# The last short unit's first layer between the last tile's layers, its second layer in two column halves

## The chip, the cores and the metric

The kernel runs on one core of one Trainium2 chip. The metric is the device time of one execution in microseconds. The times of runs are medians; the profile shows one execution, in microseconds from its first instruction.

## The reference

Two stages follow each other. The first is causal attention with a decay, for 8 batches of 8 heads with 576 positions and 64 values per head. The second is a feed-forward block over the 4608 resulting rows.

```python
def _attn_ref(q, k, v, f):                       # 8 batches, 8 heads, 576 x 64
    scores = scale * np.matmul(q, k.transpose(0, 1, 3, 2))
    cum = np.cumsum(np.log(np.clip(f, 0.0001, 1.0)), axis=-1)
    decay = cum[:, :, :, None] - cum[:, :, None, :]
    scores = np.where(causal, -1000000000.0, scores + decay)
    attn = np.exp(scores - np.max(scores, axis=-1, keepdims=True))
    attn = attn / (np.sum(attn, axis=-1, keepdims=True) + 1e-09)
    return np.matmul(attn, v)

def _moe_ref(x, w_in, w_out):                    # x: 4608 x 512, d_ff = 2048
    h = x @ w_in
    g = h * np.clip(h + 3.0, 0.0, 6.0) / 6.0
    return g @ w_out
```

## The kernel before

All matrix products of the second stage are done in float16 with each operand split into a high and a low half; a product is then three matmuls: high x high, high x low and low x high.

Attention goes head by head (64 heads, in the order of the list `VH`). The feed-forward work is cut into units that are filled in between the attention's instructions. A batch has 576 positions: 512 of them make one *tile* (`moe_tile`, 8 in all), and the 64 positions left over of two batches together make one *short unit* of 128 positions (`moe_short`, 4 in all; the unit u serves batches 2u and 2u + 1).

A tile has two layers. The first (`h_unit`, 16 times, one for each block of 128 hidden values) multiplies weights by the tile's 512 positions: 4 x 3 matmuls of 512 columns into one PSUM tile `ph`, then a relu on ScalarE, a min-and-multiply on VectorE that reads `ph` again and so frees it, a cast on ScalarE to the high half and a subtraction on VectorE to the low half. Both halves lie in `gT`. The second layer (`out_unit`, 4 times, one for each 128 positions) sums over all 16 blocks: 16 x 3 matmuls of 512 columns (lines 819, 820, 821: the first two read the high half of `gT`, the third the low half) into one PSUM tile `po`, an eviction by ScalarE into an SBUF tile `o` (line 825), and a DMA to the output on SyncE's queue (line 828).

A short unit has the same two layers at 128 positions. Its first layer (`h_short`) is done in four groups of four blocks; a group is 4 x 4 x 3 matmuls of 128 columns (lines 797 to 799) into one PSUM tile `phs`, two relus (line 805, one for each batch's half), one min-and-multiply (line 809, which frees the PSUM tile), a cast (line 811) and a subtraction (line 812). Before, it writes into columns 0 to 127 of `gT`, which the out_unit of the same positions of the tile has read. Its second layer is one out_unit, whose rows go to the output in two DMAs.

PSUM tiles for this work come from three places: two buffers of `ps_m` and one of `ps_t`, taken by a counter (`mm_tile`: every third goes to `ps_t`). There are three buffers for the results of the relu (`rt`) and two for `o`.

The order of instructions on each engine is written by the framework's planner before the run: among those that are ready it takes the lowest priority number. The units are Python generators, and `fill` draws them piece by piece, from one `yield` to the next; a piece of an out_unit is six matmuls, a piece of an h_short is 24. Each piece is drawn in a priority block of its own, with `LOW_M = 0`:

```python
while credit[0] >= 1 and units:
    with tc.high_priority(offset=-LOW_M):
        r = next(units[0], 0)
```

After the last head the list `units` still holds what is left of the seventh tile; then the eighth tile (`t` = 7) and the last short unit (`u` = 3) are put behind it by `done`, and the loop `while units: fill(1)` draws them to the end.

The tile `vst` holds the batch's v in float32 (5 x 520 values per partition). Its readers are `v_scale` and `v_split`; the last `v_split` of the last batch is called at its sixth head.

Of the kernel before, what the change touches and what calls it, by code (L numbers as in the profile page):

```python
# [9 lines left out]
F16 = mybir.dt.float16  # L10
BF16 = mybir.dt.bfloat16
F32 = mybir.dt.float32
F32R = mybir.dt.float32r
I32 = mybir.dt.int32
AF = mybir.ActivationFunctionType
# [5 lines left out]
def kernel(  # L21
# [10 lines left out]
    nc = tc.nc  # L32

    NHEAD, D, S = qk.shape
    D //= 2
    B = vS.shape[0]
    H = NHEAD // B
    NT, DM = out.shape
    DFF = w_in.shape[1]
    P = 128  # L40
# [5 lines left out]
    NFC = DFF // P  # L46
    TT = 512
# [7 lines left out]
    p2 = ctx.enter_context(tc.tile_pool(name="p2", bufs=2))  # L55
# [22 lines left out]
        out=W[:, 4 * P:], in_=W[:, 4 * P:], pattern=[[-1, P]],  # L78
# [16 lines left out]
    QA = 256  # L95
# [35 lines left out]
    vst = cpool.tile([P, NCH, VR], F32, name="vst")  # L131

    w1 = [cpool.tile([P, NCC, DFF], F16, name=f"w1{i}") for i in range(2)]
    w2 = cpool.tile([P, NFC + 1, 2, DM], F16, name="w2")
    gT = cpool.tile([P, 2, NFC, TT], F16, name="gT")
# [15 lines left out]
    NG = 4  # L151
    SC = cpool.tile([P, 80], F32, name="SC")
    SV, IV, UO, UX, A1 = 0, 8, 16, 24, 32
# [47 lines left out]
    def scol(c):  # L201
        return SC[:, c:c + 1]
# [172 lines left out]
    def moe_scale_in(b, j):  # L375
        nc.vector.scalar_tensor_tensor(
            scol(A1 + NG * b + j), scol(IV + b), CG, scol(I1 + j), op0=ALU.mult, op1=ALU.mult
        )

    def moe_scale_out(b):  # L380
        nc.vector.scalar_tensor_tensor(
            scol(UO + b), scol(IV + b), 1.0 / (6.0 * CG), scol(I1R), op0=ALU.mult, op1=ALU.mult
        )
        nc.vector.tensor_tensor(scol(UO + b), scol(UO + b), scol(I2), op=ALU.mult)
        if b % 2 == 1:
            nc.vector.tensor_copy(SC[:64, UX + b:UX + b + 1], SC[:64, UO + b - 1:UO + b])
            nc.vector.tensor_copy(SC[64:, UX + b:UX + b + 1], SC[64:, UO + b:UO + b + 1])
# [191 lines left out]
    for half in NAT:  # L579
        g = [0]  # L580
# [3 lines left out]
    o = 0  # L584
# [176 lines left out]
    def mm_tile(name, three):  # L761

        turn[0] += 1
        if three and turn[0] % 3 == 0:
            return ps_t.tile([P, TT], F32, tag="tr", name=name)
        return ps_m.tile([P, TT], F32, tag="mm", name=name)

    def h_unit(t, fc, c0, c1):
        x = xT[t % 2]
        nw = c1 - c0  # L770
        ph = mm_tile(f"ph_{t}_{fc}_{c0}", t > 0 or c0 > 0)[:, :nw]
        fs_ = slice(fc * P, (fc + 1) * P)
        for cc in range(NCC):
            xh, xl = (x[:, cc, c0 // P:c1 // P, hl] for hl in range(2))
            nc.tensor.matmul(ph, w1[0][:, cc, fs_], xh, start=(cc == 0), stop=False)  # L775
            nc.tensor.matmul(ph, w1[0][:, cc, fs_], xl, start=False, stop=False)  # L776
            nc.tensor.matmul(ph, w1[1][:, cc, fs_], xh, start=False, stop=(cc == NCC - 1))  # L777
            if cc == 1 and nw == TT:
                yield H_COST
        r = p2.tile([P, TT], F32, tag="rt", name=f"r_{t}_{fc}_{c0}", bufs=3)[:, :nw]  # L780
        nc.scalar.activation(  # L781
            r, ph, AF.Relu, bias=bias_r, scale=scol(A1 + NG * t + fc * NG // NFC)
        )
        nc.vector.scalar_tensor_tensor(r, r, 6.0 * CG, ph, op0=ALU.min, op1=ALU.mult)  # L784
        nc.scalar.copy(gT[:, 0, fc, c0:c1], r)  # L785
        nc.vector.tensor_tensor(gT[:, 1, fc, c0:c1], r, gT[:, 0, fc, c0:c1], op=ALU.subtract)  # L786
        yield H_COST

    def h_short(u, j):
        x = xS[u % 2]  # L790
        n = NFC // NG
        ph = mm_tile(f"phs_{u}_{j}", True).rearrange("p (f t) -> p f t", f=n)
        for i in range(n):
            fs_ = slice((n * j + i) * P, (n * j + i + 1) * P)
            for cc in range(NCC):
                xh, xl = (x[:, cc, :, hl] for hl in range(2))
                nc.tensor.matmul(ph[:, i], w1[0][:, cc, fs_], xh, start=(cc == 0), stop=False)
                nc.tensor.matmul(ph[:, i], w1[0][:, cc, fs_], xl, start=False, stop=False)
                nc.tensor.matmul(ph[:, i], w1[1][:, cc, fs_], xh, start=False, stop=(cc == NCC - 1))
            if i == 1:  # L800
                yield H_COST
        r = p2.tile([P, TT], F32, tag="rt", name=f"rs_{u}_{j}", bufs=3)
        r = r.rearrange("p (f t) -> p f t", f=n)
        for h in range(2):
            nc.scalar.activation(
                r[:, :, 64 * h:64 * h + 64], ph[:, :, 64 * h:64 * h + 64], AF.Relu, bias=bias_r,
                scale=scol(A1 + NG * (2 * u + h) + j),
            )
        nc.vector.scalar_tensor_tensor(r, r, 6.0 * CG, ph, op0=ALU.min, op1=ALU.mult)
        g = [gT[:, i, n * j:n * j + n, 0:P] for i in range(2)]  # L810
        nc.scalar.copy(g[0], r)  # L811
        nc.vector.tensor_tensor(g[1], r, g[0], op=ALU.subtract)
        yield H_COST

    def out_unit(s, three, col, rows_):
        po = mm_tile(f"po_{rows_[0]}", three)
        ts_ = slice(s * P, (s + 1) * P)
        for fc in range(NFC):
            nc.tensor.matmul(po, gT[:, 0, fc, ts_], w2[:, fc, 0, :], start=(fc == 0), stop=False)  # L819
            nc.tensor.matmul(po, gT[:, 0, fc, ts_], w2[:, fc, 1, :], start=False, stop=False)  # L820
            nc.tensor.matmul(po, gT[:, 1, fc, ts_], w2[:, fc, 0, :], start=False, stop=(fc == NFC - 1))  # L821
            if fc % 2 and fc < NFC - 1:
                yield 2.0 - H_COST
        o = p2.tile([P, DM], F32, tag="o", name=f"o_{rows_[0]}")
        nc.scalar.activation(o, po, AF.Copy, scale=scol(col))
        w = P // len(rows_)
        for i, r0 in enumerate(rows_):
            nc.sync.dma_start(out[r0:r0 + w, :], o[i * w:(i + 1) * w])
        yield 2.0 - H_COST

    def moe_tile(t, c0=0, c1=TT):
        for fc in range(NFC):
            j, new = divmod(fc, NFC // NG)
            if new == 0 and c0 == 0:
                while j not in w_in_done:
                    next(w_in_q, None)
                moe_scale_in(t, j)
            yield from h_unit(t, fc, c0, c1)
        if t == 0:
            for _ in wq:  # L840
                pass
        if c0 == 0:
            moe_scale_out(t)
        r0 = t * S + (64 if t else 0)
        for s in range(c0 // P, c1 // P):
            yield from out_unit(s, t > 0 or s * P >= QA, UO + t, [r0 + s * P])

    def moe_short(u):
        for j in range(NG):
            yield from h_short(u, j)  # L850
        a, b = 2 * u, 2 * u + 1
        yield from out_unit(0, True, UX + b, [b * S - 64] if a == 0 else [a * S, b * S])

# [50 lines left out]
    def queue(unit, columns):  # L904
        units.append(unit)
        left[0] += TILE * columns / TT
# [22 lines left out]
    def one(*a):  # L929
        yield from moe_tile(*a)  # L930

    def done(v):
        kind, n = VH[v]
        if kind == "A":
            if n == NPAIR - 1:
                queue(one(0, 0, QA), QA)
            return
        b, h = divmod(n, H)
        if h == H - 1:
            queue(one(b, QA if b == 0 else 0, TT), TT - QA if b == 0 else TT)  # L940
            if b % 2:
                queue(moe_short(b // 2), P)

    prev = None
# [2 lines left out]
    for i, (kind, n) in enumerate(VH):  # L947
        b, h = divmod(n, H)
        if kind == "A":
            b = h = 0  # L950
# [10 lines left out]
        if moved is not None:  # L961
            done(moved)
            moved = None
# [22 lines left out]
        if pend_x is not None:  # L986
            x_move(pend_x)
            if VH[pend_x][0] == "F":
                moved = pend_x
            else:  # L990
                done(pend_x)
            pend_x = None
# [26 lines left out]
    if moved is not None:  # L1019
        done(moved)  # L1020
# [40 lines left out]
```

## Time and profile before

| | |
|---|---|
| time of the runs, median (lowest to highest, 3 runs) | 1084.39 us (1082.83 to 1085.16) |
| time of the profiled execution | 1078.21 us |
| its span, first to last instruction | 1076.4 us |
| TensorE busy | 1012.2 us, 94% |
| VectorE busy | 731.5 us, 68% |
| ScalarE busy | 587.9 us, 55% |
| mean granted TensorE clock | 0.989 |

In the rows below, PE is TensorE's matmuls, PEld its weight loads, DVE VectorE, ACT ScalarE, POOL GpSimd and SPq the queue of SyncE. A row of an instruction in order of time has its start, its length, the engine, the line of the kernel, the tiles as output<-inputs, and in brackets the idle time before it with what ended it. A matmul's length includes its way through the array; the pace is read from start to start. In the names, numbers of buffers are left out, so `w` stands for the weights of either layer.

### The profile page before, as it was taken

To read this page: it belongs to the slowest core of one execution; us is meant where nothing else is said; L and a number is where in the kernel's file an instruction comes from. 1 tells how busy PE (TensorE), PEld (TensorE's weight loads), DVE (VectorE), ACT (ScalarE), POOL (GpSimd) and SP (SyncE) were. 2 spreads that over 40 slices of the span, in tenths; PEclk is the share of its full clock that TensorE was granted. 3 is DMA by queue.
4 is the path that set the end of the run, shared out by engine and by line. 5 is a ranking of instruction groups with operands and counts; after the bars stand their busy time and mean duration, and the time that the engine had idled before them with its cause. 6 is when DMAs were issued, how large, how long until landed. Compare 5 with 4: busy or idle time off the path is not lost.

```text
span 1076.4 us, 21155 instructions
## 1 busy us (share of the span) xinstructions
PE 1012.2 (94%) x7650; PEld 600.5 (56%) x7650; DVE 731.5 (68%) x1903; ACT 587.9 (55%) x1189; POOL 407.8 (38%) x505
## 2 busy tenths in 40 slices
PE   2889987899999999999999999999999999999995
PEld 1557854665555755555555755555555755544453
DVE  7897999996885669866865677767855678305101
ACT  4787656765664557555654557555744567225102
POOL 7353455454433444443434344543442442000000
PEclk9989989999999999999999999999999999999999
DMA  7976548966656766567465476557565654300010
GB/s 241 288 212 191 135 100 149 201 146 128 156 101 137 138 151 129 114 148 162 97 127 109 104 167 128 127 133 170 106 110 113 118 96 86 70 30 1 1 40 10
DMA packets 259140, 133.78 MB, mean 124 GB/s; under 512 B 226933, under 2 KB 228525, under 8 KB 259037
## 3 DMA queue, kind: packets, MB, share of 16 engines
q1 hardware_dynamic: 259036, 132.44, 55.6%
q8 instruction: 60, 0.98, 0.4%
q14 instruction: 44, 0.35, 0.1%
HBM read 47.93 MB, written 9.73 MB: 54 GB/s over the span
## 4 chain that ended last, share of the span: by engine, by line
PE 65%; DVE 17%; ACT 6%; issue 5%; DMA 5%; SPq 1%; POOL 1%; ACTq 0%; DVEq 0%; POOLq 0%
PE po L819 10%; PE po L821 10%; PE po L820 10%; PE ph L775 7%; PE ph L776 6%; PE ph L777 6%; DVE pp L620 3%; PE pn L609 3%; PE pn L612 3%; ACT pp L632 2%; DVE ring L649 2%; DMA vst<-in_vS_dram 2%; DVE gT L786 2%; DVE r L784 1%; DVE nb L626 1%
## 5 line engine op out<-in xcount | busy, mean ns | idle before, releaser
L820 PE MATMUL po<-w,gT 128*128 128x512 f16 x576 | 215.7, 382 | 2.5 <-DVE w L295 2.5
L819 PE MATMUL po<-w,gT 128*128 128x512 f16 x576 | 213.6, 382 | 4.1 <-ACT gT L811 3.1
L821 PE MATMUL po<-w,gT 128*128 128x512 f16 x576 | 215.7, 382 | 0.1
L632 ACT ACTIVATE pp<-pp,nb 128x192 f32<-128x192 f32 x280 | 138.9, 552 | 134.8 <-DVE nb L626 134.2
L775 PE MATMUL ph<-xT,w 128*128 128x512 f16 (+1 forms) x576 | 200.2, 358 | 7.1 <-DVE r L784 6.9
L649 DVE TENSOR_TENSOR ring<-pp,ring 128x128 f16<-128x128 f32 (+2 forms) x216 | 144.5, 678 | 83.6 <-ACT ring L646 80.8
L776 PE MATMUL ph<-xT,w 128*128 128x512 f16 (+1 forms) x576 | 199.7, 357 | 0.0
L777 PE MATMUL ph<-xT,w 128*128 128x512 f16 (+1 forms) x576 | 199.2, 357 | 0.0
L447 POOL TENSOR_SCALAR TK<-ST 64x576 fp32r<-64x576 f32 (+1 forms) x68 | 50.1, 737 | 245.2 <-PE pn L609 202.5
L620 DVE CUSTOM_DVE_ANT_0 pp<-pn,W 128x192 f32<-128x192 f32 x280 | 123.3, 482 | 24.7 <-PE pn L612 22.5
L459 POOL TENSOR_TENSOR T<-ST,T 64x576 fp32r<-64x576 f32 (+1 forms) x68 | 99.7, 1466 | 82.8 <-DMA T<-TK 74.3
L609 PE MATMUL pn<-TK,TQ 68*128 68x192 f32 x336 | 124.4, 384 | 6.3 <-issue 5.2
L784 DVE SCALAR_TENSOR_TENSOR r<-r,ph 128x512 f32<-128x512 f32 (+1 forms) x144 | 89.1, 620 | 54.6 <-ACT r L781 54.2
L785 ACT CAST gT<-r 128x512 f16<-128x512 f32 (+1 forms) x144 | 81.5, 569 | 76.9 <-DVE r L784 76.2
L786 DVE TENSOR_TENSOR gT<-r,gT 128x512 f16<-128x512 f32 (+1 forms) x144 | 102.8, 717 | 20.6 <-ACT gT L785 19.0
L781 ACT ACTIVATE r<-ph,bias_r,SC 128x512 f32<-128x512 f32 (+1 forms) x144 | 103.6, 724 | 20.7 <-PE ph L777 17.5
L646 ACT CAST ring<-pp 128x192 f16<-128x192 f32 x280 | 114.3, 449 | 0.0
L612 PE MATMUL pn<-T,T 128*128 128x192 f32 x336 | 113.0, 363 | 0.0
L456 POOL TENSOR_TENSOR T<-ST,TQ 64x576 fp32r<-64x576 f32 (+2 forms) x68 | 100.2, 1474 | 14.2 <-PE pn L612 5.3
L821 PEld LDWEIGHTS <-gT 128*128 128x128 f16 x576 | 56.5, 99 | 71.1 <-issue 9.4
L820 PEld LDWEIGHTS <-gT 128*128 128x128 f16 x576 | 56.5, 99 | 63.4 <-issue 6.4
L655 POOL TENSOR_TENSOR ring<-pp,ring 128x128 f16<-128x128 f32 x96 | 59.9, 624 | 78.2 <-ACT ring L646 33.9
(146 smaller groups left out, 1958.0 us busy)
## 6 DMA issues: line engine op xcount, KB each, us to landing
ST<-in_qk_dram SPq DMA_DIRECT2D x64, 288.0 KB
T<-TK SPq DMA_DIRECT2D x64, 144.0 KB
out_dram<-o SPq DMA_DIRECT2D x33, 256.0 KB
ring<-in_w_out_dram SPq DMA_DIRECT2D x16, 512.0 KB
T<-TQ SPq DMA_DIRECT2D x56, 144.0 KB
vst<-in_vS_dram SPq DMA_DIRECT2D x7, 1040.0 KB
ring<-in_w_in_dram SPq DMA_DIRECT2D x9, 512.0 KB
w<-in_w_in_dram SPq DMA_DIRECT2D x7, 512.0 KB
```

The source lines that it names most:

```text
L609: nc.tensor.matmul(dst, TQ[i][0:D + 4, qs], TK[i][0:D + 4, a:e], start=True, stop=False)
L612: nc.tensor.matmul(dst, T7[j][:, qs], T1[j][:, a:e], start=False, stop=True)
L620: nc.vector.tensor_tensor_reduce(pp[:r, w:w + kw], pn[:r, o:o + kw], W[:r, 4 * P + r - kw:4 * P + r], 1.0, -3.0e38, ALU.add, ALU.max, accu ...
L632: nc.scalar.activation(x_, x_, AF.Exp, bias=nb[:r, e0 + x:e0 + x + 1], scale=0.125)
L649: eng.tensor_tensor(hl[:r, a:a + c * P], pp[:r, at[c] + 64:at[c] + kw], hl[:r, h0[c] + 64:h0[c] + kw], op=ALU.subtract,)
L775: nc.tensor.matmul(ph, w1[0][:, cc, fs_], xh, start=(cc == 0), stop=False)
L776: nc.tensor.matmul(ph, w1[0][:, cc, fs_], xl, start=False, stop=False)
L777: nc.tensor.matmul(ph, w1[1][:, cc, fs_], xh, start=False, stop=(cc == NCC - 1))
L786: nc.vector.tensor_tensor(gT[:, 1, fc, c0:c1], r, gT[:, 0, fc, c0:c1], op=ALU.subtract)
L819: nc.tensor.matmul(po, gT[:, 0, fc, ts_], w2[:, fc, 0, :], start=(fc == 0), stop=False)
L820: nc.tensor.matmul(po, gT[:, 0, fc, ts_], w2[:, fc, 1, :], start=False, stop=False)
L821: nc.tensor.matmul(po, gT[:, 1, fc, ts_], w2[:, fc, 0, :], start=False, stop=(fc == NFC - 1))
```

## The change

In the last tile only, the last short unit's four h_short groups are drawn after the tile's 16 h_units and before its four out_units. They write into `vst`, seen as float16, instead of `gT`. After the four out_units follow two out_units for the short unit, each over all 16 blocks but over 256 of the 512 output columns: 48 matmuls of 256 columns, one eviction of 128x256 and two DMAs each. The last `moe_short` is no longer queued, and its columns are counted with the tile.

```diff
-    def h_short(u, j):
+    def h_short(u, j, gd):
...
-        g = [gT[:, i, n * j:n * j + n, 0:P] for i in range(2)]
+        g = [gd[:, i, n * j:n * j + n, 0:P] for i in range(2)]
...
-    def out_unit(s, three, col, rows_):
-        po = mm_tile(f"po_{rows_[0]}", three)
+    def out_unit(s, three, col, rows_, gs=None, cols=(0, DM)):
+        g = gT if gs is None else gs
+        c = slice(*cols)
+        po = mm_tile(f"po_{rows_[0]}_{cols[0]}", three)[:, c]
...
+            nc.tensor.matmul(po, g[:, 0, fc, ts_], w2[:, fc, 0, c], start=(fc == 0), stop=False)
+            nc.tensor.matmul(po, g[:, 0, fc, ts_], w2[:, fc, 1, c], start=False, stop=False)
+            nc.tensor.matmul(po, g[:, 1, fc, ts_], w2[:, fc, 0, c], start=False, stop=(fc == NFC - 1))
...
+        nc.scalar.activation(o[:, c], po, AF.Copy, scale=scol(col))
...
+            nc.sync.dma_start(out[r0:r0 + w, c], o[i * w:(i + 1) * w, c])
...
         if c0 == 0:
             moe_scale_out(t)
+        last = t == B - 1
+        if last:
+            gs = vst.bitcast(F16).rearrange("p c e -> p (c e)")[:, 0:2 * NFC * P]
+            gs = gs.rearrange("p (a f t) -> p a f t", a=2, f=NFC)
+            for j in range(NG):
+                yield from h_short(t // 2, j, gs)
         r0 = t * S + (64 if t else 0)
         for s in range(c0 // P, c1 // P):
             yield from out_unit(s, t > 0 or s * P >= QA, UO + t, [r0 + s * P])
+        if last:
+            for cols in ((0, DM // 2), (DM // 2, DM)):
+                yield from out_unit(0, True, UX + t, [(t - 1) * S, t * S], gs, cols)
 
     def moe_short(u):
         for j in range(NG):
-            yield from h_short(u, j)
+            yield from h_short(u, j, gT)
...
-            queue(one(b, QA if b == 0 else 0, TT), TT - QA if b == 0 else TT)
-            if b % 2:
+            queue(
+                one(b, QA if b == 0 else 0, TT),
+                TT - QA if b == 0 else TT + P if b == B - 1 else TT,
+            )
+            if b % 2 and b < B - 1:
                 queue(moe_short(b // 2), P)
```

More of the change, by code (lines that the diff above doesn't have):

```diff
@@ L813, in h_short @@
         yield H_COST
-    def out_unit(s, three, col, rows_):
-        po = mm_tile(f"po_{rows_[0]}", three)
+    def out_unit(s, three, col, rows_, gs=None, cols=(0, DM)):
+        g = gT if gs is None else gs
+        c = slice(*cols)
+        po = mm_tile(f"po_{rows_[0]}_{cols[0]}", three)[:, c]
         ts_ = slice(s * P, (s + 1) * P)
         for fc in range(NFC):
-            nc.tensor.matmul(po, gT[:, 0, fc, ts_], w2[:, fc, 0, :], start=(fc == 0), stop=False)
-            nc.tensor.matmul(po, gT[:, 0, fc, ts_], w2[:, fc, 1, :], start=False, stop=False)
-            nc.tensor.matmul(po, gT[:, 1, fc, ts_], w2[:, fc, 0, :], start=False, stop=(fc == NFC - 1))
+            nc.tensor.matmul(po, g[:, 0, fc, ts_], w2[:, fc, 0, c], start=(fc == 0), stop=False)
+            nc.tensor.matmul(po, g[:, 0, fc, ts_], w2[:, fc, 1, c], start=False, stop=False)
+            nc.tensor.matmul(po, g[:, 1, fc, ts_], w2[:, fc, 0, c], start=False, stop=(fc == NFC - 1))
             if fc % 2 and fc < NFC - 1:
                 yield 2.0 - H_COST
-        o = p2.tile([P, DM], F32, tag="o", name=f"o_{rows_[0]}")
-        nc.scalar.activation(o, po, AF.Copy, scale=scol(col))
+        o = p2.tile([P, DM], F32, tag="o", name=f"o_{rows_[0]}_{cols[0]}")
+        nc.scalar.activation(o[:, c], po, AF.Copy, scale=scol(col))
         w = P // len(rows_)
         for i, r0 in enumerate(rows_):
-            nc.sync.dma_start(out[r0:r0 + w, :], o[i * w:(i + 1) * w])
+            nc.sync.dma_start(out[r0:r0 + w, c], o[i * w:(i + 1) * w, c])
         yield 2.0 - H_COST
```

## The prediction

> **What bounds the kernel now.** I read the page's busy shares first, then the waits of TensorE from 900 us on, then stretches of the last 75 us, and last the instructions of those stretches in order of time.
>
> ```profile
> span 1076.4 us, 21155 instructions
> PE 1012.2 (94%) x7650; PEld 600.5 (56%) x7650; DVE 731.5 (68%) x1903; ACT 587.9 (55%) x1189; POOL 407.8 (38%) x505
> ...
> PE phs L797 <- DVE rs L809: 3.3, 1, 3.3
> PE po L819 <- ACT gT L811: 2.5, 1, 2.5
> PE po L819 <- ACT o L825: 0.8, 1, 0.8
> ```
>
> TensorE is busy for 94% of the span. The change touches only what follows the last attention head, so the question is what TensorE waits for there, and the last three rows are the whole answer: three waits, all in the last 45 us. The stretches show them with their edges (length, then TensorE busy time and number of matmuls, then the granted clock):
>
> ```profile
> 1011.90:1026.14 14.24, 14.24 (x67) 1.00 0.00 1
> 1055.20:1056.60 1.40, 1.39 (x25) 1.00 0.05 12
> ...
> 1051.80:1055.20 3.40, 0.13 (x3) 1.00 0.00 0
> 1055.20:1065.70 10.50, 10.48 (x84) 1.00 0.01 2
> 1065.70:1068.30 2.60, 0.12 (x3) 1.00 0.00 0
> 1071.40:1076.40 5.00, 0.00 (x0) 0.76 0.23 52
> ...
> L819 PE MATMUL po<-w,gT 128*128 128x512 f16 x80 | 30.0, 379 | 3.3 <-ACT gT L811 2.5 <-ACT o L825 0.8
> L797 PE MATMUL phs<-xS,w 128*128 128x128 f16 x64 | 10.3, 219 | 3.3 <-DVE rs L809 3.3
> ```
>
> The first row prices a matmul of 512 columns: its ends fall on starts, one matmul overhanging, so 14.24 us over 66 is 0.216 us. The second prices one of 128 columns: 1.40 over 25 is 0.056. The grouped rows are of 1001.35 to 1071.45, from the last tile's first second-layer matmul to the end of TensorE: lines 819, 820 and 821 run 80 times each, and 797, 798 and 799 run 64 times each. That is 240 x 0.216 + 192 x 0.056 = 51.8 + 10.7 = 62.5 us of work in 70.05 us. So about 7.5 us of idle time lie in this stretch, and 5.0 us more behind the last matmul. Where they lie:
>
> ```profile
> 1032.22 0.38 PE L821 MATMUL po<-w,gT 128*128 128x512 f16 x1
> 1032.63 1.26 ACT L825 ACTIVATE o<-po,SC 128x512 f32<-128x512 f32 x2 [28.87 <-PE po L821]
> 1033.37 0.38 PE L819 MATMUL po<-w,gT 128*128 128x512 f16 x1 [0.78 <-ACT o L825]
> 1035.45 0.69 ACT L825 ACTIVATE o<-po,SC 128x512 f32<-128x512 f32 x1 [1.56 <-DMA out_dram<-o]
> ...
> 1051.92 2.84 ACT L805 ACTIVATE rs<-phs,bias_r,SC 128x256 f32<-128x256 f32 x6 [6.58 <-PE phs L799]
> 1055.21 0.22 PE L797 MATMUL phs<-xS,w 128*128 128x128 f16 x1 [3.28 <-DVE rs L809]
> ...
> 1064.61 0.38 PE L821 MATMUL po<-w,gT 128*128 128x512 f16 x1
> 1064.82 0.22 PE L797 MATMUL phs<-xS,w 128*128 128x128 f16 x1
> 1065.61 0.22 PE L799 MATMUL phs<-xS,w 128*128 128x128 f16 x1
> 1068.31 0.39 PE L819 MATMUL po<-w,gT 128*128 128x512 f16 x1 [2.49 <-ACT gT L811]
> 1068.54 0.38 PE L820 MATMUL po<-w,gT 128*128 128x512 f16 x1
> 1069.04 0.39 PE L821 MATMUL po<-w,gT 128*128 128x512 f16 x1
> ```
>
> Three things are to be seen. (a) At 1032.4 the first three second-layer tiles (three PSUM tiles are all there are) are done together, and the fourth waits for the first eviction: 1033.37 less (1032.22 + 0.216) is 0.93 us. (b) At 1051.8 six ACTIVATEs in one row, two for each group, say that groups 0, 1 and 2 of the short unit's first layer ended together; all PSUM tiles were full, and group 3 had to wait for a relu and a multiply: 3.4 us. (c) The last 15 matmuls of group 3 run only after the short unit's second layer used up groups 0 to 2; its last quarter then waits 2.6 us for group 3's chain, and line 821 about 0.3 us more for the low half (start to start 1068.54 to 1069.04 instead of 0.216). Together 0.93 + 3.4 + 2.6 + 0.3 = 7.2, near the 7.5 of the balance. The reason for the lockstep is in the code: each piece between two yields is drawn in a priority block of its own, so pieces number their instructions from the same value and the planner runs equal ones in turn.
>
> **The change, part by part.**
>
> ```profile
> 1065.86 1.03 ACT rs L805 x2
> 1066.91 0.70 DVE rs L809
> ...
> 999.03 0.78 ACT L781 ACTIVATE r<-ph,bias_r,SC 128x512 f32<-128x512 f32 x1 [0.44 <-PE ph L777]
> 1001.62 0.78 ACT L781 ACTIVATE r<-ph,bias_r,SC 128x512 f32<-128x512 f32 x1 [0.44 <-PE ph L777]
> ```
>
> First layer moved ahead of the second. The 192 small matmuls, 8 ACTIVATEs, 4 casts and 8 VectorE operations stay as many; they issue no DMA and pass no queue of SP or POOL. They now follow the last h_unit, where PSUM tiles come free one by one, 2.59 us apart (1001.62 less 999.03), and not all at once. A group is 48 x 0.056 = 2.7 us, so groups run nearly one behind another, and a tile needs 1.03 + 0.70, some 1.75 us, from a group's last matmul to its release: covered by the next group where they run singly, bare once where two end together. So wait (b) lies between 0 and 3.4 us; I take 1.75, one bare chain, since the cadence is about a group's length and ties stay likely. Saved: 1.65.
>
> Wait (c) goes. The short unit's second layer now has the tile's four out_units in front, 192 x 0.216 = 41 us, against a chain of under 4 us (1065.86 to 1069.04). If that cover were gone, the 2.9 us would be back. Saved: 2.9. The new place gs is v's tile; the last reader of v is two heads earlier, so nothing waits on it: 0.
>
> Wait (a) I keep at 0.93: three tiles of the second layer again run in turn. It is 0 if they drift apart, and about 1.9 if a second round of three (the last out_unit and the two halves) repeats it. Saved: 0.
>
> Two halves instead of one. No 256-column matmul of line 819 exists; the first tile's first layer has the shape:
>
> ```profile
> 99.91 0.27 PE L777 MATMUL ph<-xT,w 128*128 128x256 f16 x1
> 100.56 0.27 PE L777 MATMUL ph<-xT,w 128*128 128x256 f16 x1
> ...
> L825 ACT ACTIVATE o<-po,SC 128x512 f32<-128x512 f32 x36 | 24.4, 683 | 109.4 <-PE po L821 107.9 <-DMA out_dram<-o 1.6
> L781 ACT ACTIVATE r<-ph,bias_r,SC 128x256 f32<-128x256 f32 x32 | 17.5, 560 | 6.4 <-PE ph L777 3.2 <-DVE gT L786 2.5 <-DVE r L784 0.4
> L781 ACT ACTIVATE r<-ph,bias_r,SC 128x512 f32<-128x512 f32 x112 | 86.1, 772 | 14.3 <-PE ph L777 14.3
> ```
>
> Six starts apart, 0.65 us: 0.108 each, a weight load before every one. So 96 x 0.108 = 10.4 us against 48 x 0.216 = 10.4: no cost, and the 48 more weight loads lie beside matmuls. The bound above is a half that costs as much as a whole matmul, a rival below. The first half's eviction and two DMA issues lie beside the second half's 5.2 us of matmuls.
>
> The end:
>
> ```profile
> 1071.41 0.69 ACT L825 ACTIVATE o<-po,SC 128x512 f32<-128x512 f32 x1 [3.15 <-PE po L821]
> 1072.12 1.15 SPq L828 DMA_DIRECT2D out_dram<-o  x2
> ```
>
> Eviction 0.69, two issues 1.15, then landing and closing until 1076.4. A half's eviction should save 0.2 (772 against 560 ns for the same halving on line 781). Its DMAs move half the bytes: between 0 and 0.6 us less, as the 16 engines were busy for 0.23 of the 5.0 us; I take 0.1. Saved: 0.3. The other end of this term is a loss: only two `o` tiles exist, and if the last out_unit and both halves end together, the third eviction waits for a DMA as it did from 1032.63 to 1035.45: 2.8 us more.
>
> Sum: 1.65 + 2.9 + 0 + 0 + 0.3 = 4.85 us. The profiled execution took 1078.21 us, 1.8 around its span; it would become 1073.4. The median shown is 1084.39, 6.2 above it, and I carry the difference over: 1079.5.
>
> **The rivals.** *All waits go*: groups run singly and tiles drift apart, (a) and (b) vanish too: 4.85 + 1.75 + 0.93 = 7.5, so 1076.9. The 2.59 us cadence speaks for it, the ties of equal priorities against.
>
> *The waits come back elsewhere*: three groups again end together (3.4 kept), (a) stays, and the last three evictions queue at the end (2.8 lost): 2.9 + 0.2 - 2.8 = 0.3, so 1084.1. For it: the same lockstep twice in this trace. Against it: PSUM tiles here come free singly.
>
> *The change does not do what it says*: the planner still holds first-layer groups back behind second-layer pieces, as it did with the 15 matmuls at 1064.82, and group 3 is late again: 0, so 1084.4. Against it: they now take their PSUM tiles first.
>
> *Slower: the halves pay for their weight loads.* If a half matmul with its load took as long as a whole one, 0.216, the two halves would cost 96 x 0.108 = 10.4 us more: 1079.5 + 10.4 = 1089.9. It decides from 0.108 + 4.85 / 96 = 0.159 us a matmul on. Against it stand 0.108 for the shape and 0.056 for half of it, both with a load each. The Trainium skill's page "TensorE: Matmul & The Clock Gate", section "Back-to-back issue gap", says that streams of weight load and matmul settle at about 81 ns at 128 columns, not at the 56 of a matmul by itself; 25 ns more on 96 matmuls would be an estimated 2.4 us, and the sum 2.45 instead of 4.85. This trace disagrees, with 56 ns in a stream that loads weights for each.
>
> *Slower: the clock falls after a wait.* If the 3.4 us wait (b) stays whole and TensorE then ran for as long at half speed, 1.7 us are lost on top of the second rival: 1085.8. Against it: in the stretch after the 3.40 us gap the granted clock is 1.00 and the pace 0.056. The same page, section "What's actually happening", has the clock halved after an idle window of about 3.4 us; by that rule this gap stood at its edge, and the trace shows no fall here.
>
> **How the numbers follow.** Forecast 0.60, all waits go 0.18, waits come back 0.10, no effect 0.04, weight loads 0.05, clock 0.03. A measurement of this kernel tells about 0.2%, 2.2 us, from no change. Faster: 0.60 + 0.18, less 0.01 for forecasts that fall short, 0.77; same 0.15; slower 0.08. The forecast's own range goes with (b) from 0 to 3.4: 1077.7 to 1081.2. The whole range takes in the first rival with the end's 0.6 and the spread of the runs, 1076.0, and the second rival, 1084.2; what is left out is the slower ones.
>
> **What would show it.** Right: the six ACTIVATEs of line 805 in one row are gone, TensorE's wait for line 811 is gone, TensorE's idle time from the last h_unit to the last matmul is near 2.7 us, 96 matmuls of 128x256 stand 0.108 apart, and the last eviction is near 0.5 us. Wrong: a wait of 3 us or more of a first-layer group for line 809, three evictions behind the last matmul with one released by a DMA, or halves further apart than 0.108 us.

## The result and the profile after

The changed kernel takes 1078.32 us in the median of 5 runs (1076.77 to 1080.35), the kernel before 1084.39 (1082.83 to 1086.21, 5 runs): a ratio of 0.9942, interval 0.9924 to 0.9960. Both kernels were timed once more later, on one chip, in 12 runs each, beside 35 runs of the kernel before (median 1079.86): the changed kernel 1077.63, ratio 0.9972 [0.9954, 0.9991]; the kernel before against itself 1082.56, ratio 1.0016 [0.9997, 1.0036]. So the gain is there both times, 6.1 us the first time and 2.2 us the second (4.9 if the repeat of before is taken instead of the 35 runs). Runs of one kernel lie far apart: the kernel before alone ran from 1075.48 to 1087.09 us on that chip. Between the two timings the kernel before moved from 1084.39 to 1079.86 us, the changed one only from 1078.32 to 1077.63.

The head of the page, and then TensorE's waits from 985 us on (total, times, longest):

```profile
span 1078.6 us, 21257 instructions
PE 1013.8 (94%) x7698; PEld 604.8 (56%) x7698; DVE 726.8 (67%) x1903; ACT 587.9 (55%) x1190; POOL 408.5 (38%) x505
```

```profile
PE po L821 <- DVE rs L809: 4.6, 2, 2.8
```

This execution took 1080.35 us and is longer than the profiled one of before, 1078.21, though the median fell. The two spans may not be subtracted: the order of instructions on every engine is the same in both kernels up to the last h_unit, and yet its last relu (line 781) starts at 1004.56 us here and at 1001.62 before. That is variation ahead of the change. What can be compared is the stretch from that relu to the end of the span: 74.8 us before, 74.0 after. I call it the tail; the experiments are read by it too.

The change moves line numbers: the lines 819 to 821, 825 and 828 of before are 821 to 823, 827 and 830 here. Three waits of 6.6 us in all have become two of 4.6. Both are in the rows of VectorE, ScalarE and TensorE (start, duration, instruction, and in brackets the idle time before and who ended it):

```profile
1012.60 2.85 ACT L805 ACTIVATE rs<-phs,bias_r,SC 128x256 f32<-128x256 f32 x6 [5.89 <-PE phs L799]
1015.31 0.58 PE L821 MATMUL po<-w,gT 128*128 128x512 f16 x1 [2.80 <-DVE rs L809]
1016.11 0.63 PE L823 MATMUL po<-w,gT 128*128 128x512 f16 x1
1016.54 0.63 PE L821 MATMUL po<-w,gT 128*128 128x512 f16 x1
...
1033.97 0.69 ACT L827 ACTIVATE o<-po,SC 128x512 f32<-128x512 f32 x1 [16.87 <-PE po L823]
1037.87 0.22 PE L797 MATMUL phs<-xS,w 128*128 128x128 f16 x1
1038.07 0.69 ACT L827 ACTIVATE o<-po,SC 128x512 f32<-128x512 f32 x1 [3.41 <-PE po L823]
1059.07 1.26 ACT L827 ACTIVATE o<-po,SC 128x512 f32<-128x512 f32 x2 [20.31 <-PE po L823]
...
1064.70 0.22 PE L797 MATMUL phs<-xS,w 128*128 128x128 f16 x1
1064.76 0.22 PE L798 MATMUL phs<-xS,w 128*128 128x128 f16 x1
1064.81 0.22 PE L799 MATMUL phs<-xS,w 128*128 128x128 f16 x1
1066.12 0.69 DVE L809 SCALAR_TENSOR_TENSOR rs<-rs,phs 128x512 f32<-128x512 f32 x1 [47.86 <-ACT rs L805]
1066.86 0.27 PE L821 MATMUL po<-w,vst 128*128 128x256 f16 x1 [1.83 <-DVE rs L809]
```

Six relus in one row at 1012.60: groups 0 to 2 ended together again, and TensorE stood for 2.80 us. Then group 3 was not finished. Ten of its 48 matmuls ran between the out_units (one at 1037.87), 35 in one go when the last two out_units were done, and the last three at 1064.70, behind 36 matmuls of the short unit's first half. The 35 in one go, as the share of the tile `phs` in a stretch of TensorE (length, then busy time and matmuls, granted clock, DMA share, GB/s):

```profile
1058.50:1061.00 2.50, 2.12 (x35) 1.00 0.15 57
```

The multiply that frees group 3's PSUM tile ended at 1066.81 (1066.12 + 0.69), and TensorE stood for 1.83 us until the second half could have it. In between, out_units ran two at a time (evictions at 1033.97 and 1038.07, then two in one row): group 3 held the third PSUM tile through all of it.

The first rows also show something else: behind the 2.80 us wait the matmuls of 512 columns start 0.43 us apart, twice the 0.216 of before. TensorE's stretches, with the same columns:

```profile
1004.30:1012.50 8.20, 8.20 (x145) 1.00 0.01 2
1012.50:1015.30 2.80, 0.00 (x1) 0.94 0.00 0
1015.30:1019.00 3.70, 3.69 (x11) 0.58 0.00 0
1019.00:1022.00 3.00, 3.00 (x18) 1.00 0.00 0
...
1064.90:1066.85 1.95, 0.13 (x3) 1.00 0.00 0
...
1073.60:1078.60 5.00, 0.00 (x0) 0.78 0.22 52
```

The granted clock is 0.58 over the 3.70 us behind the wait, so about 3.70 x 0.42 = 1.6 us of work were lost there. In the profile of before, the clock behind a wait of 3.40 us was 1.00.

The halves, as a group of instructions and then in order of time, and the end:

```profile
L821 PE MATMUL po<-w,vst 128*128 128x256 f16 x32 | 8.4, 272 | 1.8 <-DVE rs L809 1.8
```

```profile
1066.97 0.27 PE L822 MATMUL po<-w,vst 128*128 128x256 f16 x1
...
1072.85 0.47 ACT L827 ACTIVATE o<-po,SC 128x256 f32<-128x256 f32 x1 [5.38 <-PE po L823]
1073.61 0.47 ACT L827 ACTIVATE o<-po,SC 128x256 f32<-128x256 f32 x1 [0.29 <-PE po L823]
1073.35 2.43 SPq L830 DMA_DIRECT2D out_dram<-o  x4
```

Half matmuls start 0.11 us apart, and an eviction of 256 columns takes 0.47 us. But the halves, too, ran partly in turn and ended 0.76 us apart, so SyncE's queue issued four DMAs in one row of 2.43 us where before two took 1.15. From the start of the last eviction to the end of the span it is 1078.6 less 1073.61, 4.99 us, as it was before (1076.4 less 1071.41, 4.99).

### The profile page after: what moved, and what is told of

It reads as the page before. It is cut to its first block, busy times and chain, and to the rows that moved or that the text cites. A ratio compares the mean times of both kernels' runs of the same rounds, so it can differ in the third digit from the quotient of the medians.

```text
span 1078.6 us, 21257 instructions
## 1 busy us (share of the span) xinstructions
PE 1013.8 (94%) x7698; PEld 604.8 (56%) x7698; DVE 726.8 (67%) x1903; ACT 587.9 (55%) x1190; POOL 408.5 (38%) x505
## 4 chain that ended last, share of the span: by engine, by line
PE 66%; DVE 13%; DMA 6%; ACT 6%; issue 5%; POOL 2%; SPq 1%; ACTq 0%; DVEq 0%; POOLq 0%
PE po L821 10%; PE po L822 10%; PE po L823 10%; PE ph L775 7%; PE ph L776 7%; PE ph L777 7%; DVE pp L620 3%; PE pn L609 3%; PE pn L612 3%; DMA vst<-in_vS_dram 2%; ACT pp L632 2%; DVE ring L649 2%; DVE gT L786 1%; DVE r L784 1%; DMA ring<-in_w_out_dram 1%
## 5 line engine op out<-in xcount | busy, mean ns | idle before, releaser
L821 PE MATMUL po<-w,gT 128*128 128x512 f16 x560 | 208.0, 383 | 5.2 <-DVE rs L809 2.8
L822 PE MATMUL po<-w,gT 128*128 128x512 f16 x560 | 210.2, 383 | 1.3 <-DVE w L295 1.3
L775 PE MATMUL ph<-xT,w 128*128 128x512 f16 (+1 forms) x576 | 201.5, 359 | 10.3 <-DVE r L784 10.1
L823 PE MATMUL po<-w,gT 128*128 128x512 f16 x560 | 210.1, 382 | 0.0
L649 DVE TENSOR_TENSOR ring<-pp,ring 128x128 f16<-128x128 f32 (+2 forms) x216 | 140.4, 660 | 82.6 <-ACT ring L646 81.6
L823 PEld LDWEIGHTS <-gT 128*128 128x128 f16 x560 | 55.0, 99 | 68.3 <-issue 9.2
L822 PEld LDWEIGHTS <-gT 128*128 128x128 f16 x560 | 54.9, 99 | 63.5 <-issue 8.5
```

What stands on the lines that cost most here:

```text
L649: eng.tensor_tensor(hl[:r, a:a + c * P], pp[:r, at[c] + 64:at[c] + kw], hl[:r, h0[c] + 64:h0[c] + kw], op=ALU.subtract,)
L821: nc.tensor.matmul(po, g[:, 0, fc, ts_], w2[:, fc, 0, c], start=(fc == 0), stop=False)
L822: nc.tensor.matmul(po, g[:, 0, fc, ts_], w2[:, fc, 1, c], start=False, stop=False)
L823: nc.tensor.matmul(po, g[:, 1, fc, ts_], w2[:, fc, 0, c], start=False, stop=(fc == NFC - 1))
```

## The experiments

Two questions: which part of the change carries the gain, and why the waits are still there. My theory was that the equal numbers of the priority blocks make the pieces run in turn and so make every one of these waits, wherever the unit stands; the rivals were that the place or the halves matter by themselves, and that the clock behind a wait does.

**Both kernels again.** No edit.

> The kernel before once more, unchanged. Two theories on why the medians are 6.1 us apart while the two profiled executions differ by only 0.7 us behind the last relu of the last tile's first layer (74.8 us before, 74.0 after). Clock theory: the wait of 3.4 us behind the short unit's first groups mostly drops TensorE's clock to a half for a window of 3.4 us, and the profiled execution of before happened to escape it; then executions of 1083 to 1086 us show a lower mean granted clock than the 0.989 of the one that took 1078.2 (each window at half lowers the mean by 0.0016 and costs up to 1.7 us, so 0.984 to 0.987), and this profile has a stretch at half clock behind that wait. Drift theory: the stages before the last tile differ by some us from execution to execution for reasons of DMA or start; then the granted clock is near 0.989 in slow and fast executions alike, and the last relu of the first layer stands 4 to 6 us later than at 1001.6 with the same 74.8 us behind it. By both, the ratio to before is 1.000 within 0.002.

> The changed kernel once more, unchanged. By both theories its ratio to before is again 0.992 to 0.996. Clock theory: executions with a granted clock of 0.985 are some 2 to 4 us slower than those with 0.989. Drift theory: no such order. The stretch from the last relu of the first layer to the end is 72.3 us where the clock stays up behind the 2.8 us wait, 74.0 where it falls to a half for one window.

The times stand above. The repeat of before has the waits of before, to a tenth, but another clock. The first matmul behind wait (b), and then TensorE's stretches:

```profile
1055.90 0.26 PE L797 MATMUL phs<-xS,w 128*128 128x128 f16 x1 [3.29 <-DVE rs L809]
```

```profile
1055.50:1061.40 5.90, 5.50 (x38) 0.50 0.01 3
...
1068.40:1071.70 3.30, 0.82 (x16) 1.00 0.00 0
1071.70:1075.10 3.40, 3.40 (x9) 0.50 0.00 0
```

Behind wait (b), 3.29 us here, TensorE ran at half clock until 1061.4, and behind wait (c) for 3.4 us more. 5.50 x 0.5 + 3.40 x 0.5 = 4.5 us; the tail is 78.9 us instead of 74.8, 4.1 longer. The repeat of the changed kernel has a tail of 74.1 and, as the first profile, lost clock behind its 2.80 us wait (0.63 over 3.7 us). So the same wait, in the same kernel, is followed by half clock in one execution and by full clock in another.

Both theories hold in part. The two executions of before differ by the clock: the last relu starts at 1002.29 us in the repeat, only 0.7 us later than at 1001.62, and 4.1 of the 4.8 us between the spans lie in the tail. The two of after differ by drift: the relu starts at 1004.56 and at 1001.78, with tails of 74.0 and 74.1. Of the 47 runs of before on this chip, the 19 with a granted clock of 0.985 or less have a median of 1082.5 us, the 16 with 0.988 or more one of 1079.8; runs of like clock still lie several us apart. The ratio of the changed kernel, 0.9972, is outside the 0.992 to 0.996 that both theories gave.

**The first layer alone in the new place**, the second layer whole:

```diff
-            for cols in ((0, DM // 2), (DM // 2, DM)):
-                yield from out_unit(0, True, UX + t, [(t - 1) * S, t * S], gs, cols)
+            yield from out_unit(0, True, UX + t, [(t - 1) * S, t * S], gs)
```

> The first layer of the last short unit ahead of the last tile's second layer, in v's place, as in the change, but its second layer whole, 48 matmuls of 512 columns and one eviction of 128x512. If the halves carry the gain at the end, this loses it: an eviction of 0.69 instead of 0.47 us and two DMAs of 128 KB instead of 64 KB, 0.3 us in all; against that the wait of 1.8 us between the halves goes, or becomes the wait of the last 12 matmuls for the last group, 2.6 us. By the wait theory it is within 1.5 us of the changed kernel, ratio to before 0.992 to 0.997. If the move of the first layer brings nothing, 1.000.

1079.04 us in 12 runs, ratio 0.9979 [0.9959, 0.9999]: by the times not to be told from the whole change beside it (0.9972), and just outside the 0.992 to 0.997 expected. Its waits, and group 3's relus:

```profile
PE po L821 <- DVE rs L809: 2.8, 1, 2.8
PE po L821 <- ACT vst L811: 2.5, 1, 2.5
```

```profile
1062.75 1.02 ACT L805 ACTIVATE rs<-phs,bias_r,SC 128x256 f32<-128x256 f32 x2 [8.58 <-PE phs L799]
```

Group 3 is late here as well, and wait (c) is back at its old size. The tail is 73.4 us, with the clock at 1.00 behind the 2.8 us wait; that of after, less the 1.6 us of lost clock, is 72.4. The 1.0 us between them is what the halves save at wait (c), 2.5 + 0.3 against 1.83.

**The halves alone**, the first layer in its old place and in `gT`: `moe_short` draws the two half out_units in place of one.

> The first layer of the last short unit in its old place behind the last tile's out_units, in gT, its second layer in two halves of 256 columns. The halves are ready to run in turn with the first-layer groups, so both end together, and group 3 is again late: the wait of 3.4 us stays, the one of 2.6 us stays at about that, and two evictions and four DMAs queue behind the last matmul. By the wait theory no gain, 0 to +1 us, ratio 0.999 to 1.002. If the halves are what brings the gain, 0.994.

1082.59 us in 12 runs, ratio 1.0015 [0.9992, 1.0037]: nothing that can be told from no change. Its waits, and its end:

```profile
PE phs L797 <- DVE rs L809: 3.3, 1, 3.3
PE po L821 <- ACT gT L811: 2.5, 1, 2.5
PE po L821 <- ACT o L827: 0.8, 1, 0.8
```

```profile
1070.77 0.84 ACT L827 ACTIVATE o<-po,SC 128x256 f32<-128x256 f32 x2 [3.07 <-PE po L823]
1071.27 2.43 SPq L830 DMA_DIRECT2D out_dram<-o  x4
```

All three waits are those of before. The two halves ended together, and their four DMA issues stood in one row again. The tail is 75.5 us, 0.7 longer than in the first profile of before, and that lies at the end: 1076.5 less 1070.77 is 5.7 us, against 4.99. So what gain there is comes with the move, not with the halves by themselves.

**The order numbered through.** In three kernels (before, first layer alone, after) the units that are left behind the last head are drawn outside the priority blocks, so that each piece has higher numbers than the one before it. Against the same kernel in the old order nothing else is changed:

```diff
+    tail = [False]
...
-            with tc.high_priority(offset=-LOW_M):
+            with nullcontext() if tail[0] else tc.high_priority(offset=-LOW_M):
                 r = next(units[0], 0)
...
+    tail[0] = True
     while units:
         fill(1)
```

> The kernel before, without the change, with its last units numbered through in the same way. Lockstep theory: the short unit's groups run one behind another after the tile's out_units, the last quarter of its second layer has 36 matmuls (7.8 us) in front as cover for group 3's chain of 3.1 us, and all three waits go without any move: 67 to 68 us from the last relu of the first layer to the end instead of 74.8 to 78.9, ratio 0.990 to 0.994. Theory that the place matters (the last group is late because nothing follows it): the wait of 2.6 us for group 3 stays, 70 us.

> As the changed kernel with units numbered through, but with the short unit's second layer whole instead of in two halves. With no lockstep left this shows the halves alone: by the rows of the profiles an eviction of 0.47 instead of 0.69 us and DMAs of half the size at the end, 0.3 to 0.5 us in favour of the halves between last matmul and end; the time itself is within 0.2% of the version with halves. If the halves cost something on TensorE, the stretch of matmuls is longer there.

> The changed kernel, but the last units are drawn outside the priority blocks, so that their instructions are numbered through and the planner runs piece after piece instead of equal pieces in turn. Lockstep theory (the waits come from groups and tiles that end together, and the half clock from the waits): groups 0 to 3 run one behind another, the waits of 2.8 and 1.8 us go, and with them the stretch at half clock behind the first; from the last relu of the tile's first layer to the end 67 us instead of 74.0, ratio to before 0.990 to 0.994. Rival, that three PSUM tiles are too few in any order (a group of 2.7 us against a chain of 1.75 us and evictions of 0.7): waits of 1 to 3 us stay and the stretch is 71 to 73 us, ratio near 0.997.

| kernel | us, median (runs) | ratio to before | tail, us |
|---|---|---|---|
| before, in order | 1071.11 (6) | 0.9902 [0.9883, 0.9921] | 67.5 |
| first layer moved, in order | 1070.85 (5) | 0.9897 [0.9880, 0.9915] | 67.5 |
| after, in order | 1071.88 (6) | 0.9913 [0.9896, 0.9930] | 67.0 |

The kernel before ran beside them at 1081.44 us (17 runs). All three are about 10 us faster than before, and their intervals overlap; they are also below the 1077.63 and 1078.32 us of the changed kernel, which were taken in other sessions. What TensorE's lane looks like with the old place and the new order (evictions and relus on ScalarE, then one stretch of TensorE):

```profile
1012.40 0.69 ACT L825 ACTIVATE o<-po,SC 128x512 f32<-128x512 f32 x1 [8.15 <-PE po L821]
1022.76 0.69 ACT L825 ACTIVATE o<-po,SC 128x512 f32<-128x512 f32 x1 [9.67 <-PE po L821]
...
1046.16 1.02 ACT L805 ACTIVATE rs<-phs,bias_r,SC 128x256 f32<-128x256 f32 x2 [1.94 <-PE phs L799]
1048.84 1.02 ACT L805 ACTIVATE rs<-phs,bias_r,SC 128x256 f32<-128x256 f32 x2 [0.29 <-PE phs L799]
```

```profile
1002.00:1064.30 62.30, 62.30 (x433) 1.00 0.05 18
```

Evictions come singly, 10.36 us apart (48 x 0.216), relus in pairs 2.68 us apart (48 x 0.056), and TensorE is busy for all of the 62.30 us. No wait is left, although not one instruction was moved to another unit. The tail is 74.8 - 67.5 = 7.3 us shorter: the 7.2 us of idle time that the prediction counted. Against the repeat of before, with its lost clock, it is 78.9 - 67.5 = 11.4; the 10.3 us between the medians lie between the two. The new order also differs ahead of the tail, from 952.8 us on, but there was nothing to gain there: TensorE is busy for all of 900 to 1000 us in the profile of before. The halves have their use only here: in after, in order, the last eviction starts 5.24 us behind the one before it, with two issues behind it instead of four:

```profile
1063.28 0.47 ACT L827 ACTIVATE o<-po,SC 128x256 f32<-128x256 f32 x1 [4.55 <-PE po L823]
1068.52 0.47 ACT L827 ACTIVATE o<-po,SC 128x256 f32<-128x256 f32 x1 [4.77 <-PE po L823]
1069.02 1.10 SPq L830 DMA_DIRECT2D out_dram<-o  x2
```

It is 1072.9 less 1068.52, 4.4 us to the end, 0.6 to 0.7 less than with the whole out_unit (1069.3 less 1064.26, 5.04); 0.3 to 0.5 was expected. Its times do not show that (1071.88 against 1070.85).

**A long wait put in.** After, in order, with nine ScalarE copies of block 0 of `gT` onto itself behind the first layer, so that TensorE has to wait for a known time at a known place; their scale is a 1.0 worked out from group 3's result, which keeps them behind it.

```diff
+            one_ = p2.tile([P, 1], F32, tag="m1", name="one_")
+            nc.vector.tensor_scalar(one_, gs[:, 0, NFC - 1, 0:1], 0.0, 1.0, op0=ALU.mult, op1=ALU.add)
+            for _ in range(9):
+                nc.scalar.activation(gT[:, 0, 0], gT[:, 0, 0], AF.Copy, scale=one_)
```

> The changed kernel numbered through, with one wait put in on purpose: behind the short unit's first layer, nine copies in a row on ScalarE of the tile's first block onto itself, for which the tile's second layer must wait. The wait is 2.4 + 0.2 + 9 x 0.6, about 8 us. Clock theory: a wait that long holds at least one whole window of 3.4 us, so the clock falls every time, and the matmuls behind it run at half pace (0.43 us for 512 columns) for one window: 1.7 us, or 3.4 for two, on top of the wait; stretch to the end 67 + 8 + 1.7 to 3.4 = 77 to 78.5 us. If waits cost their own length alone, 75 us and a pace of 0.216 behind it.

The wait, and TensorE's stretches around it:

```profile
PE po L821 <- ACT gT L855: 10.1, 1, 10.1
```

```profile
1011.60:1021.60 10.00, 0.00 (x0) 0.65 0.00 1
1021.60:1024.90 3.30, 3.24 (x8) 0.50 0.02 5
1024.90:1028.30 3.40, 3.40 (x17) 0.99 0.00 0
```

The wait became 10.1 us and not 8: the nine copies took 6.75 us, 0.75 each instead of 0.6, and the first began 3.25 us after TensorE stopped. The clock fell while TensorE still stood (0.65 on the mean of the wait) and stayed at half for the 3.30 us behind it, about 1.65 us of work lost. 10.1 + 1.65 = 11.7; the tail is 78.5 us, 11.5 above that of after, in order, and the median, 1083.75 us (12 runs, ratio 1.0021 [1.0001, 1.0040]), 11.9 above. That the clock fell is seen in the one profiled execution; the granted clock of the 12 runs, 0.979 to 0.987 against 0.985 to 0.992 in the six of after, in order, fits a fall in the others.

## Why the prediction came out, step by step

The forecast was 1079.5 us; 1078.32 was measured, with a sum of 4.85 against a measured 6.1 (and 2.2 the second time). The sign and about the size came, but not by the steps named, and that the time fell into the range is luck: the stretch that the change touches became 0.8 us shorter in the two profiled executions, not 4.85. The 6.2 us that the forecast added were the distance of one profiled execution from the median of three runs, and the second timing puts that median 4.5 us lower. Of the five signs that were to show it right, two are missing: the six ACTIVATEs still stand in one row, and TensorE's idle time is 4.6 us instead of 2.7. Idle time as the brackets of the rows give it, before and after:

| term | forecast saving | measured |
|---|---|---|
| (b) three groups end together | 1.65 (3.4 to 1.75) | 0.5 (3.28 to 2.80) |
| (c) group 3 late | 2.9 (to 0) | 1.0 (2.49 + 0.3 to 1.83) |
| (a) fourth out_unit waits for an eviction | 0 | 0.8 (0.78 to 0) |
| halves on TensorE | 0 | 0 (0.11 us each) |
| the end | 0.3 | 0 (4.99 and 4.99) |
| clock behind a wait | 0 | -1.6 |

0.5 + 1.0 + 0.8 - 1.6 = 0.7, and the tail is 0.8 us shorter, so these terms account for it.

*The step that failed first is "PSUM tiles come free one by one" in (b).* They do, but the pieces of the three groups were drawn in blocks of equal numbers, and 144 matmuls of three groups in turn took from 1004.3 to 1012.5, all groups ending with the last. The cadence of the release says when a group may begin, not when it ends. I had written that the lockstep is in the code and had then priced (b) by half of it.

*"Wait (c) goes"* failed in the same way. The cover, 41 us of out_units, was there; group 3 was simply not run under it, which is what the rival "the change does not do what it says" told of. Its counter-argument, that the groups now take their PSUM tiles first, was right on the tile and wrong on the work: group 3 began in its tile at 1021.35 us and kept it until 1066.81, and at 1058.8 it still had 38 of its 48 matmuls to run. *Wait (a)* went for the same reason, not forecast: with one PSUM tile held, only two out_units run in turn, and 35 of group 3's matmuls, about 2 us of work, stand beside the evictions of the last two.

*The halves* came as worked out: 0.11 us a matmul with a load each. So the slower rival, halves that pay for their weight loads, is out. The 81 ns at 128 columns of the Trainium skill's page "TensorE: Matmul & The Clock Gate", section "Back-to-back issue gap", is not what the trace shows behind the change either: 56 ns (rows 1064.70 to 1064.81). *The end* had its price wrong: the eviction shrank by 0.22 us, as forecast, but the two issues of the first half stood ahead of the second half's on the queue. I had said that they lie beside 5.2 us of matmuls; that holds only when the halves run one after the other.

*The clock.* I gave the fall 0.03 since the trace of before showed none behind 3.4 us. One execution was too little to say so: of three profiles with a wait of 3.3 us at (b) one has it (the repeat of before), of three with a 2.8 us wait two (both of after). The length does not decide alone. What does can be read from the traces. Within one execution the edges of the stretches at half clock lie whole multiples of 3.41 us apart (in the repeat of before at 1054.65, 1061.47, 1071.71 and 1075.13 us), and where this grid lies differs from one execution to the next. In the first profile of before the clock falls at 1074.03, behind the last matmul, which gives its grid. Wait (b) in these windows, first in before, then in its repeat:

```profile
1050.14:1053.55 3.41, 1.79 (x33) 1.00 0.00 0
1053.55:1056.96 3.41, 1.75 (x28) 1.00 0.02 5
```

```profile
1051.23:1054.65 3.42, 1.38 (x25) 1.00 0.00 0
1054.65:1058.06 3.41, 2.16 (x21) 0.50 0.02 5
```

In before the wait lies across an edge, with 1.62 and 1.66 us of idle time in two windows, and the clock stays. In the repeat 2.04 us of it lie in one window, and the next one is at half. The longer waits of the other profiles fall out in the same way, by the most idle time that they put into one window: 1.53 us (first layer alone), 1.83 (the second wait in the repeat of after) and 2.00 (halves alone) with full clock behind; 2.44 and 2.49 (the first wait in the two profiles of after), 2.48 (wait (c) in the repeat of before) and 3.10 (the long wait) with half. So in these tails the border lies at about 2.0 us of idle time in a window, an estimate from these cases; no run moved one wait against the grid on purpose. Earlier in the span a window with 1.58 us fell as well (at 276.4 us in the repeat of before), so idle time by itself may not be the whole rule. The Trainium skill's page "TensorE: Matmul & The Clock Gate", section "What's actually happening", says that the unit that grants the clock looks at windows of some 3.4 us that run freely, whatever the kernel does. The traces agree, with edges 3.41 us apart and another place of the grid in each execution; but a window did not have to be idle all through, 2.04 us were enough.

What the change is worth by itself: without the loss of clock the tail of after would be 74.0 - 1.6 = 72.4, against 74.8, some 2.4 us. With the lost clock left in, the tails of the two profiles of each kernel are 76.9 and 74.1 us in the mean, 2.8 apart; in the second timing the changed kernel is 2.9 us below the median of all 47 runs of before (1080.57). These agree, though two profiles of each kernel are few. That the first timing gave 6.1 I can only argue: an execution of before can lose over 4 us to the clock in its tail and one of after 1.6, and the stretch ahead of the tail varies by several us in any kernel (its end lies between 999.91 and 1005.90 us in ten profiles). How the 6.1 divides between these is open.

## What to carry to other kernels

When several tiles are finished in one row and the next one waits, look first at how the order is numbered, and only then at where the work stands: here the move and the split kept most of the waits, and numbering the pieces through removed all of them without a move, for 10 us against the change's 2 to 6. A unit that holds a PSUM tile and is not being run can make a later one wait, here 1.83 us at the end. And compare stretches that begin at the same instruction, not spans: the spans of the two profiled executions had the wrong sign.

## What the hardware did unexpectedly

TensorE's clock fell to half behind waits as short as 2.80 us, and not behind some of 3.3. In these tails it fell where a wait put 2.04 us or more of idle time into one window of a 3.41 us grid, and not where it put 2.00 us or less there. The place of the grid differs between executions, so the same wait costs different times. Behind 2.80 us the clock was at half for one window, behind the 3.29 us of the repeat for two. The price was some 1.55 and 1.7 us of work in the two profiles of the changed kernel (0.5 x 3.09 and 0.5 x 3.41 us of busy time at half clock), and in the repeat of before 4.5 us for two waits, 2.8 of it behind the one of 3.29. A wait of this size on TensorE thus costs its length and, in some executions, half of that or more again.
